# A linear-attention and token-selection kernel: q columns grouped by heads, and M in six passes

## The chip, the cores and the metric

The kernel runs on one core of one Trainium2 chip. The core has a matrix engine (TensorE, "PE" in the profile; its weight loads are listed as "PEld"), VectorE ("DVE"), ScalarE ("ACT"), GpSimd ("POOL"), and SyncE ("SP"), whose queue here issues most of the transfers (DMAs). Each engine works through its own instructions in the order in which they were written, and waits for others by semaphores. The metric is the device time of one execution in microseconds (us).

## The reference, cut to what matters

x holds 2048 tokens of 640 bfloat16 numbers. Three things are added: x, a linear attention A on the normalised x, and a block B that changes eight tokens only.

```python
xn = layernorm(x)
# A: 32 heads of 20 columns, wqkv is 640 x 1920, wo is 640 x 640
q, k, v = split_heads(xn @ wqkv)
phi = lambda t: where(t > 0, t + 1, exp(t)) + 1e-6
pq, pk = phi(q), phi(k)
kv  = einsum("bhsd,bhse->bhde", pk, v)      # 20 x 20 per head
z   = einsum("bhsd->bhd", pk)               # column sums
num = einsum("bhqd,bhde->bhqe", pq, kv)
den = einsum("bhqd,bhd->bhq", pq, z) + 1e-6
A = (num / den) @ wo
# B: the 8 tokens with the largest r = x @ w_r
y = (silu(x_sel @ w_gate) * (x_sel @ w_up)) @ w_down * sigmoid(r_sel)
B = x + scatter_add(y)
out = x + A + B
```

## The kernel before

The 2048 tokens are 16 tiles of 128. All of x stays on chip (x_sb), and so do the normalised tiles (xn), their transposes (xnT, features on the partitions), the feature maps pk (tokens on the partitions) and pqT (features on the partitions).

**The tile loop.** For each tile t TensorE computes k(t) (`k_mm`, L236, ten matmuls, with the router's column r appended to the weights), then a part of G = xn^T pk for the tile before (`ga_mm`, L259: three chunks of xn by 512 columns of pk), then q(t) (`q_mm`, L248). q comes out transposed: 25 matmuls of 128 columns have a slice of the weights as the stationary operand, `wq[:, kc, m::KC]`, every fifth column. So the 640 columns of q are dealt to five blocks m by their remainder modulo 5, and each block has four columns of each of the 32 heads. ScalarE takes exp and relu of the results (L213, L216), and VectorE combines them to phi (`phi_vec`, L225).

VectorE also takes the statistics of a later tile (`ln_stats`, L163 and L167), and normalises one (`ln_norm`, L191). From tile 4 on (LN_FAST), the small arithmetic between the two is GpSimd's: an add, two powers and a copy of one column (L171, L176, L178, L179). In iteration 5 (CATCH) statistics are taken for two tiles and two tiles are normalised, so that from there on a tile is normalised three iterations ahead of its use. From tile 3 on (PE_TR) a normalised tile is transposed by a DMA on SP's queue (L196). In VectorE's queue an iteration stands in the order: statistics, normalise, phi of q(t-1), phi of k(t).

GpSimd also makes small constants, spread over the iterations by `small_consts` (L306 to L321, and the masks of iteration 6 by `head_select`, L146 and L150). The loads of the later weights are spread over the iterations by `late_loads` (L343).

**Between the loop and the output.** Column sums z of pk (`z_mm`, L460) go through a small DMA onto the partitions; the rest of G follows (`gb1`, L489; `gb2`, L590). The top eight tokens are found by VectorE (candidates candm, pc on TensorE, then positions), gathered by GpSimd (xsT), and sent through B's matrices (gu, L606; py, L688). `pden` (L571) multiplies pqT by the masked z; its inverse rden goes to memory and comes back repeated on all partitions (rb), and `norm` multiplies pqT by it (L632). Then kv per block of 80 columns (`kv_mm`, `kv_evict`, L659 and L670) is written into kvT masked by heads, and M = kv wo is computed (L728): five blocks m, each with two halves of the output columns, two blocks of 80 accumulated one upon the other, and four head groups side by side in the array.

**Output.** For each tile ten matmuls of pqT by M (L743), then VectorE adds x_sb (L751), which has been written to memory (xcp), had y added there by an indirect DMA, and been read back. The result is stored by SP's or ScalarE's queue.

All orders are written out by hand; nothing is rescheduled.

Of the kernel before, what the change touches and what calls it, by code (L numbers as in the profile page):

```python
# [8 lines left out]
P = 128  # L9
# [16 lines left out]
PAD = 16  # L26
# [3 lines left out]
WARM = 10  # L30
LAST = (0, 320, 512, 640)
# [13 lines left out]
def kernel(  # L45
# [42 lines left out]
    wq = sb([P, KC, D], BF16, "wq")  # L88
    wv = sb([P, KC, D], BF16, "wv")
# [3 lines left out]
    kvT = sb([EB, PAD + NEB * KC * 2 * PAD], BF16, "kvT")  # L93
# [4 lines left out]
    rscr = dram.tile([NTB * P, TBLK], BF16, name="rscr")  # L98
# [55 lines left out]

    head_select(headg[:], [(0, NTB), (-4, H)], 1, 4)
# [87 lines left out]

    def q_mm(t, tag="B"):
        ps = pair(tag, f"q{t}")
        for m in range(KC):
            for kc in range(KC):
                nc.tensor.matmul(  # L248
                    ps[:, m * P : (m + 1) * P],
                    lhsT=wq[:, kc, m::KC],  # L250
                    rhs=xnT[:, kc, t * P : (t + 1) * P],
                    start=(kc == 0 and m in (0, 4)), stop=(kc == KC - 1),
                    skip_group_check=True,
                )
        return ps
# [47 lines left out]
    def small_consts(t):  # L303
        if t == 3:
            for j in range(4):
                nc.gpsimd.affine_select(  # L306
                    out=cmask[:], in_=cmask[:], compare_op=ALU.not_equal, fill=1.0,
                    base=-32 * j, pattern=[[-1, C]], channel_multiplier=1,
                )
        elif t == 4:  # L310
            nc.gpsimd.affine_select(
                out=selm[:], in_=selm[:], compare_op=ALU.not_equal, fill=1.0,
                base=0, pattern=[[-1, NTB]], channel_multiplier=1,
            )
# [26 lines left out]
    def late_loads(t):  # L341
        def part(dst, src, a, b):
            nc.sync.dma_start(dst[:, a:b, :], src[:, a:b, :])  # L343

        wv_v = wqkv_v[:, :, 2 * D : 3 * D]
        plan = {
            2: (x_sb, x_v, 8, 12), 5: (x_sb, x_v, 12, 16),
            6: (wg, kcF, 0, 2), 7: (wg, kcF, 2, 4), 8: (wg, kcF, 4, 5),
            9: (wu, kcU, 0, 2), 10: (wu, kcU, 2, 4), 11: (wu, kcU, 4, 5),
            12: (wv, wv_v, 0, 2), 13: (wv, wv_v, 2, KC), 14: (wo, wo_v, 0, 4), 15: (wo, wo_v, 4, 8),  # L350
            16: (wd, kcD, 0, 6), 17: (wd, kcD, 6, 12),
        }
        if t in plan:
            part(*plan[t])

# [12 lines left out]
    def q_phi(t, er):  # L368
        phi_vec(pqT[:, :, t * P : (t + 1) * P], er, True)
# [31 lines left out]
    for t in range(2, T):  # L401
# [18 lines left out]
        small_consts(t)  # L420
        late_loads(t)
# [20 lines left out]
    nc.vector.max(cand[:, 0, :], rT[:])  # L442
    nc.vector.max_index(idxu[:], cand[:, 0, :], rT[:])
# [28 lines left out]
    zpart = sb([P, D], F32, "zpart", tag="rb")  # L472
    nc.scalar.copy(zpart[:], zp[:, 0:D])
    zrel = sb([P, 4, KC], F32, "zrel")
    with nc.allow_non_contiguous_dma(reason="column sums from rows to partitions"):
        for i in range(4):
            (nc.sync if i < 3 else nc.scalar).dma_start(
                zrel[:, i, :], zpart[32 * i : 32 * i + 1, :].rearrange("o (p m) -> o p m", m=KC)
            )
    late_loads(T)  # L480
    late_loads(T + 1)
# [25 lines left out]
    for t in range(4, T):  # L507
        gb1(t)
# [22 lines left out]
    q_phi(T - 1, qer)  # L531
# [4 lines left out]
    for c in range(C):  # L536
# [7 lines left out]
        out=zm[:], in0=headg[:, 0, :].unsqueeze(1).to_broadcast([P, KC, H]),  # L544
# [19 lines left out]
    keep(T - 4, T)  # L564
    nc.scalar.copy(GT[:, 3:5, 0:TBLK], two(gbA[:]))
# [15 lines left out]
    nc.scalar.activation(rden[:], lden[:], AF.Exp, scale=-1.0)  # L581

# [20 lines left out]
    for a, w in enumerate((wg, wu)):  # L603
# [9 lines left out]
    sg = sb([P, FJ], F32, "sg")  # L613
# [5 lines left out]
    rb = sb([P, S], BF16, "rb")  # L619

    nc.sync.dma_start(
        rscr[:].rearrange("(p r) n -> p r n", r=4), rden[:].unsqueeze(1).to_broadcast([P, 4, TBLK])
    )
    for j in (0, 2):
        nc.sync.dma_start(
            rb[:, j * TBLK : (j + 2) * TBLK].rearrange("p (j n) -> p j n", j=2),
            rscr[j * P : (j + 2) * P, :].rearrange("(j p) n -> p j n", j=2),
        )

    def norm(j):  # L630
        sl = pqT[:, :, j * TBLK : (j + 1) * TBLK]
        nc.vector.tensor_tensor(  # L632
            out=sl, in0=sl,
            in1=rb[:, j * TBLK : (j + 1) * TBLK].unsqueeze(1).to_broadcast([P, KC, TBLK]),
            op=ALU.mult,
        )

    for t in range(2, 12):
        gb2(t)
# [8 lines left out]
    for t in range(12, T):  # L648
        gb2(t)
    nc.scalar.copy(GT[:, :, TBLK:D], gbC[:, 0:D].rearrange("p (c f) -> p c f", c=KC))  # L650


    pkv = (bank("D0", "pkv0"), bank("D1", "pkv1"), pair("B", "pkv2"))
    groups = ((0, 2, 4), (1, 3, 5), (6, 7))

    def kv_mm(i):
        for n, b in enumerate(groups[i]):
            for kc in range(KC):
# [8 lines left out]
    def kv_evict(i):  # L667
        n, w = len(groups[i]), KC * 2 * PAD
        lo, step = groups[i][0], groups[i][1] - groups[i][0]
        nc.vector.tensor_tensor(  # L670
            out=kvT[:, PAD : PAD + NEB * w].rearrange("e (b m c) -> e b m c", b=NEB, m=KC)[
                :, lo : groups[i][-1] + 1 : step, :, 0:PAD
            ],
            in0=pkv[i][0:EB, 0 : n * EB].rearrange("e (b c m) -> e b m c", b=n, m=KC),
            in1=mask80[:].rearrange("e m h j -> e m (h j)").unsqueeze(1).to_broadcast([EB, n, KC, PAD]),
            op=ALU.mult,
        )

    for i in range(3):
        kv_mm(i)  # L680
        kv_evict(i)
    norm(0)

# [19 lines left out]

    M = sb([P, KC, D], BF16, "M", tag="wq")
# [17 lines left out]
    for m in range(KC):  # L722
        pm = Acc("CBADC"[m], f"M{m}")
        for a, b in halves:
            for i in range(2):
                for g in range(4):
                    o = PAD + ((2 * g + i) * KC + m) * 2 * PAD - i * PAD
                    nc.tensor.matmul(  # L728
                        pm.at(a, b)[32 * g : 32 * g + 32, :],
                        lhsT=kvT[:, o : o + 2 * PAD],  # L730
                        rhs=wo[:, 2 * g + i, a:b],
                        start=(i == 0), stop=(i == 1),
                        tile_position=(0, 32 * g),
                    )
        copy = nc.vector.tensor_copy if m in (2, 4) else nc.scalar.copy
# [5 lines left out]

    def out_mm(t, ps, m, a, b):
# [4 lines left out]
            start=(m == 0), stop=(m == KC - 1),  # L747
# [5 lines left out]
    for t in range(T):  # L753
        o_t = work.tile([P, D], BF16, tag=("ek", "rk", "eq", "rq")[t % 4], name=f"o_t{t}")
        if t < T - 1:
            po = Acc("BADC"[t % 4], f"o{t}")
            for m in range(KC):
# [5 lines left out]
            if t == 4:  # L763
                norm(3)
        else:
            for i in range(3):
                a, b = LAST[i : i + 2]
                ps = pair("CBA"[i], f"o_last{i}")[:, 0 : b - a]
                for m in range(KC):
# [37 lines left out]
```

## Time and profile before

| | us |
|---|---|
| runs, median of 3 (lowest, highest) | 111.76 (111.65, 112.45) |
| the profiled execution's own time | 111.62 |
| its span in the profile | 109.9 |
| TensorE busy | 105.5 |
| VectorE busy | 86.1 |
| ScalarE busy | 55.1 |
| GpSimd busy | 37.9 |

How to read it: times in the trace count from the start of the span; the 1.7 us between span and time lie around it. Matmuls overlap in the engine's pipeline, so that the busy time of TensorE says only that something was in it, and the chain of work that ended last tells more: it is followed back from the last instruction, at each step to whatever released it, and shows on which engine each stretch of the time was spent. The granted TensorE clock is 1.00 in all stretches.

### The profile page before, as it was taken

How to read it: one execution, taken by the hardware profiler on the slowest of the kernel's cores; microseconds unless marked ns; L12 is line 12 of the kernel's file. 1: busy time of each engine (PE TensorE's matmuls, PEld its weight loads, DVE VectorE, ACT ScalarE, POOL GpSimd, SP SyncE). 2: the span in 40 equal slices, each digit the busy share in tenths (PEclk: the TensorE clock that was granted, in tenths of full speed). 3: DMA queues.
4: the chain of work that ended last, by engine and by line, in shares of the span. 5: the costliest groups of instructions: out<-in, count | busy, mean ns of one | idle time of the engine just before them, and what ended most of it. 6: DMA issues, size and time to landing. Idle time of an engine off the chain costs nothing.

```text
span 109.9 us, 2999 instructions
## 1 busy us (share of the span) xinstructions
PE 105.5 (96%) x1183; PEld 69.3 (63%) x1183; DVE 86.1 (78%) x205; ACT 55.1 (50%) x102; POOL 37.9 (34%) x83
## 2 busy tenths in 40 slices
PE   6998999999999999999999999999999999999990
PEld 2456866777577766777667744447995555555560
DVE  6889999887999889875999896951348967698680
ACT  4037987778867797777977745068028000000000
POOL 5414195989889955770000000240008100000000
DMA  2998164930569999998859970899541289997333
GB/s 72 335 375 292 33 36 75 283 66 3 118 177 321 220 267 280 316 305 224 290 187 285 292 257 5 232 378 372 175 145 51 15 228 323 340 387 277 128 119 119
DMA packets 25358, 23.09 MB, mean 210 GB/s; under 512 B 10624, under 2 KB 24064, under 8 KB 25344
## 3 DMA queue, kind: packets, MB, share of 16 engines
q1 hardware_dynamic: 22784, 20.43, 66.5%
q10 hardware_dynamic: 2384, 2.43, 6.4%
q8 instruction: 9, 0.15, 0.6%
q0 software_dynamic: 176, 0.04, 0.6%
q14 instruction: 5, 0.04, 0.1%
HBM read 14.94 MB, written 5.81 MB: 189 GB/s over the span
## 4 chain that ended last, share of the span: by engine, by line
PE 76%; DVE 10%; POOL 8%; issue 3%; DVEq 0%; POOLq 0%
PE o L743 14%; PE k L236 13%; PE q L248 13%; PE gbA L489 6%; PE gaC L259 5%; PE warm L271 4%; PE gbC L590 4%; POOL sq L176 3%; DVE st L163 2%; PE gaD L259 2%; DVE pk L225 2%; PE M L728 2%; POOL sc L178 2%; DVE xn L191 2%; PE gu L606 2%
## 5 line engine op out<-in xcount | busy, mean ns | idle before, releaser
L248 PEld LDWEIGHTS <-wq 128*128 128x128 bf16 x400 | 24.2, 117 | 3.4
L236 PE MATMUL k<-wk,xnT 128*128 128x512 bf16 (+1 forms) x160 | 24.8, 301 | 0.3 <-ACT xnT L206 0.3
L248 PE MATMUL q<-xnT,wq 128*128 128x128 bf16 x400 | 24.9, 220 | 0.0
L743 PEld LDWEIGHTS <-pqT 128*128 128x128 bf16 x165 | 12.8, 98 | 9.3
L236 PEld LDWEIGHTS <-xnT 128*128 128x128 bf16 x160 | 12.3, 98 | 8.5 <-ACT xnT L206 0.9
L213 ACT ACTIVATE eq<-q 128x640 bf16<-128x640 f32 x16 | 11.2, 703 | 10.5 <-PE q L248 10.5
L225 DVE SCALAR_TENSOR_TENSOR pk<-ek,rk 128x640 bf16<-128x640 bf16 x16 | 13.2, 824 | 3.6 <-ACT rk L216 3.4
L743 PE MATMUL o<-M,pqT 128*128 128x512 bf16 x110 | 15.8, 300 | 0.0
L176 POOL TENSOR_TENSOR sq<-sq,half 128x1 bf16<-128x1 bf16 x16 | 12.5, 778 | 6.2 <-DVE sc L175 4.0
L163 DVE BATCH_NORM_STATS2 st<-x_sb 128x6 f32<-128x320 bf16 x32 | 14.1, 480 | 0.4 <-DMA x_sb<-in_A_x_dram 0.4
L225 DVE SCALAR_TENSOR_TENSOR pqT<-eq,rq 128x640 bf16<-128x640 bf16 x16 | 13.2, 823 | 0.7 <-ACT rq L216 0.7
L213 ACT ACTIVATE ek<-k 128x640 bf16<-128x640 f32 x16 | 11.3, 705 | 1.6 <-PE k L236 0.4
L751 DVE TENSOR_TENSOR o_t<-o,x_sb 128x640 bf16<-128x640 f32 x11 | 8.8, 820 | 3.3 <-DMA x_sb<-xcp 1.7
L216 ACT ACTIVATE rq<-q 128x640 bf16<-128x640 f32 x16 | 11.2, 700 | 0.0
L216 ACT ACTIVATE rk<-k 128x640 bf16<-128x640 f32 x16 | 11.2, 699 | 0.0
L259 PE MATMUL gaC<-pk,xn 128*128 128x512 bf16 x32 | 9.5, 378 | 0.2 <-DVE pk L225 0.2
L537 POOL COPY xsT<-xnT 128x5 bf16 x8 | 1.9, 312 | 21.7 <-DVE icol L551 21.7
L178 POOL TENSOR_TENSOR sc<-sq,neg 128x1 f32<-128x1 bf16 x12 | 8.6, 716 | 0.9
L191 DVE TENSOR_SCALAR xn<-x_sb,sc 128x640 bf16<-128x640 bf16 (+2 forms) x17 | 6.9, 412 | 1.2 <-POOL sc L179 1.0
L489 PE MATMUL gbA<-pk,xn 128*128 128x512 bf16 x32 | 7.3, 380 | 0.0
L360 DVE TENSOR_TENSOR x_sb<-x_sb,xn 128x640 bf16<-128x640 bf16 x16 | 7.0, 482 | 0.0
L259 PEld LDWEIGHTS <-xn 128*128 128x128 bf16 x48 | 4.0, 97 | 4.1 <-issue 0.4
(152 smaller groups left out, 120.4 us busy)
## 6 DMA issues: line engine op xcount, KB each, us to landing
xcp<-x_sb SPq DMA_DIRECT2D x4, 640.0 KB, 5.2
x_sb<-in_A_x_dram SPq DMA_DIRECT2D x3, 640.0 KB, 4.7
wd<-in_B_w_down_dram SPq DMA_DIRECT2D x2, 960.0 KB, 6.6
x_sb<-xcp SPq DMA_DIRECT2D x3, 640.0 KB, 6.8
wg<-in_B_w_gate_dram SPq DMA_DIRECT2D x2, 768.0 KB, 6.6
wu<-in_B_w_up_dram SPq DMA_DIRECT2D x2, 768.0 KB, 5.3
out_dram<-o_t ACTq DMA_DIRECT2D x8, 160.0 KB, 2.7
out_dram<-o_t SPq DMA_DIRECT2D x7, 160.0 KB, 3.4
```

What stands on the lines that cost most here:

```text
L163: nc.vector.bn_stats(out=stat[t][:, h, :], in_=x_sb[:, t, h * HW : (h + 1) * HW])
L176: nc.gpsimd.tensor_tensor(out=sq[:, 1:2], in0=sq[:, 0:1], in1=half[:], op=ALU.pow)
L178: nc.gpsimd.tensor_tensor(out=sc[:, 1:2], in0=sq[:, 1:2], in1=neg1[:], op=ALU.pow)
L191: nc.vector.tensor_scalar(out=xn[:, t, a:b], in0=x_sb[:, t, a:b], scalar1=sc[:, 0:1], scalar2=sc[:, 1:2], op0=ALU.subtract, op1=ALU.mult,)
L213: nc.scalar.activation(e[:], ps[:, 0:D], AF.Exp)
L216: nc.scalar.activation(r[:], ps[:, 0:D], AF.Relu)
L225: nc.vector.scalar_tensor_tensor(out=dst, in0=ea, scalar=1.0, in1=ra, op0=ALU.min, op1=ALU.add)
L236: nc.tensor.matmul(ps[:, a:b], lhsT=xnT[:, kc, t * P : (t + 1) * P], rhs=wk[:, kc, a:b], start=(kc == 0), stop=(kc == KC - 1),)
L248: nc.tensor.matmul(ps[:, m * P : (m + 1) * P], lhsT=wq[:, kc, m::KC], rhs=xnT[:, kc, t * P : (t + 1) * P], start=(kc == 0 and m in (0, 4)) ...
L259: nc.tensor.matmul(gaC[:, c * TBLK : (c + 1) * TBLK] if c < 2 else gaD[:], lhsT=xn[:, t, c * P : (c + 1) * P], rhs=pk[:, t, 0:TBLK], start ...
L489: nc.tensor.matmul(gbA[:, (c - 3) * TBLK : (c - 2) * TBLK], lhsT=xn[:, t, c * P : (c + 1) * P], rhs=pk[:, t, 0:TBLK], start=(t == 0), stop ...
L743: nc.tensor.matmul(ps, lhsT=pqT[:, m, t * P : (t + 1) * P], rhs=M[:, m, a:b], start=(m == 0), stop=(m == KC - 1),)
```

## The change

The columns of q are dealt to the five blocks in another way. Of each head's 20 columns the first 8 go to main block c = 0, the next 8 to c = 1, each of 256 columns (32 heads), and the last 4 to a block of 128: 512 + 128 columns in a fixed order, which `regroup` describes as a view of 640 columns. Blocks 0 and 2 of pqT then belong to heads 0 to 15, blocks 1 and 3 to heads 16 to 31, and block 4 to all.

- q of tiles 0 to 6 (QTOK = 7) is computed with the tokens on the partitions, ten matmuls with the regrouped view of wq as moving operand. Its feature map pq is transposed by a DMA on SP's queue into pqT. Tiles 7 to 15 are computed transposed as before, from wqp, a regrouped copy of wq that GpSimd makes in iterations 2 to 6, two copies each.
- M in six passes: blocks 0 to 3 take one pass each, since each block has its heads in four blocks of 80 columns, and block 4 takes two. Before, each of five blocks took two.
- The head mask of z is now headm, made by selects in iterations 7 to 11; mask80 is smaller.
- The loads of the weights are in other iterations (wg from 3 on, wd in 10 and 11).
- The phi of the last q stands ahead of `max_index`. `pden` stands ahead of the last three tiles of gb1. gb2 is split: four chunks of nine tiles, then the first half of kv and py, then the other seven tiles and the fifth chunk.
- rden goes to memory once, and twelve loads repeat its rows (three for each quarter of the tokens); `norm` is two operations.
- The first four output tiles are copied out by ScalarE and then added to x_sb.

```diff
+    def regroup(ap):
+        v = ap.rearrange("p (h e) -> p h e", e=DH)
+        main = v[:, :, 0 : 2 * E8].rearrange("p h (c d) -> p c h d", c=2)
+        return (main, 0, TBLK), (v[:, :, 2 * E8 : DH], TBLK, D)
+
+    def wq_regroup(kc):
+        for src, a, b in regroup(wq[:, kc, :]):
...
+            nc.gpsimd.tensor_copy(wqp[:, kc, a:b].rearrange(pat, **kw), src)
...
     def q_mm(t, tag="B"):
         ps = pair(tag, f"q{t}")
-        for m in range(KC):
-            for kc in range(KC):
+        if t >= QTOK:
...
+                        lhsT=wqp[:, kc, m * P : (m + 1) * P],
+                        rhs=xnT[:, kc, t * P : (t + 1) * P],
...
+        for kc in range(KC):
+            for rhs, a, b in regroup(wq[:, kc, :]):
                 nc.tensor.matmul(
-                    ps[:, m * P : (m + 1) * P],
-                    lhsT=wq[:, kc, m::KC],
-                    rhs=xnT[:, kc, t * P : (t + 1) * P],
...
+                    ps[:, a:b],
+                    lhsT=xnT[:, kc, t * P : (t + 1) * P],
+                    rhs=rhs,
+                    start=(kc == 0), stop=(kc == KC - 1),
                 )
...
-            head_select(mask80[:], [(0, KC), (-DH, 4), (0, 4)], 1, DH)
+            head_select(mask80[:], [(-DH, 4), (0, E8)], 1, DH)
+        elif 7 <= t < 11:
+            m = t - 7
+            head_select(headm[:, m, m % 2, :], [(-E8, HV)], 1, E8)
+        elif t == 11:
+            head_select(headm[:, 4].rearrange("p i x -> p (i x)"), [(-E4, H)], 1, E4)
...
     def q_phi(t, er):
-        phi_vec(pqT[:, :, t * P : (t + 1) * P], er, True)
+        if t >= QTOK:
+            phi_vec(pqT[:, :, t * P : (t + 1) * P], er, True)
+            return
+        pq = work.tile([P, D], BF16, tag="pq", name=f"pq{t}", bufs=3)
+        phi_vec(pq[:], er, False)
+        nc.sync.dma_start_transpose(pqT[:, :, t * P : (t + 1) * P], pq[:])
...
         small_consts(t)
+        if 2 <= t < 2 + KC:
+            wq_regroup(t - 2)
         late_loads(t)
...
     nc.vector.max(cand[:, 0, :], rT[:])
+    q_phi(T - 1, qer)
...
-    for t in range(4, T):
+    for t in range(4, DEN_AT):
         gb1(t)
...
     nc.scalar.activation(rden[:], lden[:], AF.Exp, scale=-1.0)
+    for t in range(DEN_AT, T):
+        gb1(t)
+    nc.scalar.copy(GT[:, 3:5, 0:TBLK], two(gbA[:]))
...
-    for m in range(KC):
-        pm = Acc("CBADC"[m], f"M{m}")
-        for a, b in halves:
-            for i in range(2):
+    for m, tag, copy in (
+        (0, "C", nc.scalar.copy), (2, "A", nc.vector.tensor_copy), (1, "B", nc.scalar.copy),
+        (3, "D", nc.scalar.copy), (4, "C", nc.vector.tensor_copy),
+    ):
+        pm = Acc(tag, f"M{m}")
+        for x in (None,) if m < 4 else (0, 1):
+            for a, b in halves:
                 for g in range(4):
```

More of the change, by code (lines that the diff above doesn't have):

```diff
@@ L647, with kv_mm @@
     )
[L648 to L658, printed above, removed]
+    pkv = bank("D0", "pkv0"), bank("D1", "pkv1")
+    def kv_mm(i, ns, kcs=range(KC)):
+        for n in ns:
+            b = 4 * i + n
+            for kc in kcs:
                 nc.tensor.matmul(
@@ L667, in kv_evict @@
     def kv_evict(i):
[L668 to L682, printed above, removed]
+        src = pkv[i][0:EB, 0 : 4 * EB].rearrange("e (b h c) -> e b h c", b=4, h=4)
+        main = kvT[:, 256 * i : 256 * (i + 1)].rearrange("e (b c h d) -> e c b h d", b=4, c=2, h=4)
+        rest = kvT[:, 512 + 128 * i : 512 + 128 * (i + 1)].rearrange("e (b x) -> e b x", b=4)
+        for c in range(3):
+            w = E8 if c < 2 else E4
+            dst = main[:, c] if c < 2 else rest[:, :, 0:16].rearrange("e b (h d) -> e b h d", h=4)
+            nc.vector.tensor_tensor(
+                out=dst, in0=src[:, :, :, c * E8 : c * E8 + w],
+                in1=mask80[:, :, 0:w].unsqueeze(1).to_broadcast([EB, 4, 4, w]), op=ALU.mult,
+            )
+    kv_mm(0, range(4))
+    kv_evict(0)
     py = pair("A", "py")
@@ L702 @@
         nc.sync.dma_start(x_sb[:, a:b, :], xcp_v[:, a:b, :])
+    for t in range(GB_A, T):
+        gb2(t, gbC, range(4))
+    nc.scalar.copy(GT[:, 0:4, TBLK:D], gbC[:, 0:TBLK].rearrange("p (c f) -> p c f", c=4))
+    gbB = pair("B", "gbB")
+    for t in range(T):
+        gb2(t, gbB, (4,))
+    nc.scalar.copy(GT[:, 4, TBLK:D], gbB[:, 0:P])
+    norm(0)
+    kv_mm(1, (0, 1))
+    kv_mm(1, (2, 3), range(4))
+    kv_mm(1, (2, 3), (4,))
+    kv_evict(1)
     M = sb([P, KC, D], BF16, "M", tag="wq")
@@ L768 @@
                 ps = pair("CBA"[i], f"o_last{i}")[:, 0 : b - a]
-                for m in range(KC):
+                for m in M_ORDER:
                     out_mm(t, ps, m, a, b)
```

165 lines of the change are left out of this document (101 added, 64 removed).

## The prediction

> **What bounds the kernel now.** I read the page's shares first, then the chain that ended last in order of time, then the engine that the chain passes through before it turns to TensorE for good.
>
> ```profile
> PE 105.5 (96%) x1183; PEld 69.3 (63%) x1183; DVE 86.1 (78%) x205; ACT 55.1 (50%) x102; POOL 37.9 (34%) x83
> ...
> PE 76%; DVE 10%; POOL 8%; issue 3%; DVEq 0%; POOLq 0%
> ```
>
> TensorE sets the end, yet POOL, busy for a third of the span, holds 8% of the chain. The chain shows where:
>
> ```profile
> 27.29 0.15 POOL sc L179
> ...
> 27.47 0.45 DVE xn L191
> 27.92 0.73 DVE pqT L225
> 28.65 0.75 DVE pk L225
> ...
> 29.44 0.59 PE gaC L259 x2
> ...
> 33.67 1.40 PE q L248 x25
> 35.07 1.38 PE k L236 x10
> ```
>
> From 29.44 on TensorE works without a gap (the last two rows are q(7) and k(8); a tile is q 1.40, k 1.38, ga about 0.65: 3.43 us). Just before, it waited: POOL finishes the scale of tile 8 (sc), VectorE normalises tile 8, and only behind that, in VectorE's queue, come q's feature map and pk of tile 5, for which ga(5) waits. So in the first seven tiles POOL has no slack. Its own timeline (start, duration, operation, idle time before):
>
> ```profile
> 17.36 0.41 POOL L179 CAST sc<-mv 128x1 f32<-128x1 bf16 x1
> 18.86 0.30 POOL L171 TENSOR_SCALAR sq<-mv 128x1 bf16<-128x1 bf16 x1 [1.09 <-DVE mv L167]
> 19.24 1.00 POOL L176 TENSOR_TENSOR sq<-sq,half 128x1 bf16<-128x1 bf16 x1
> ...
> 25.98 0.57 POOL L176 TENSOR_TENSOR sq<-sq,half 128x1 bf16<-128x1 bf16 x1
> ...
> 27.26 0.18 POOL L179 CAST sc<-mv 128x1 f32<-128x1 bf16 x1
> ...
> 30.51 0.30 POOL L171 TENSOR_SCALAR sq<-mv 128x1 bf16<-128x1 bf16 x1 [0.43 <-DVE mv L167]
> ...
> 32.57 0.18 POOL L179 CAST sc<-mv 128x1 f32<-128x1 bf16 x1
> 32.71 0.43 POOL L146 TENSOR_SCALAR_AFFINE_SELECT mask<-mask 80x80 bf16<-80x80 bf16 x1
> 33.21 0.62 POOL L150 TENSOR_SCALAR_AFFINE_SELECT mask<-mask 80x80 bf16<-80x80 bf16 x1
> ```
>
> Between 18.86 and 33.83 POOL idles once, for 0.43 us.
>
> **The change, part by part.** *Regrouped weight copy.* Five pairs of POOL copies (128x512 and 128x128) stand behind the small constants of iterations 2 to 6. Pair 0 comes ahead of the scale of tile 6, pairs 1 and 2 ahead of tile 8's, pair 3 ahead of tile 10's, pair 4 behind the masks of iteration 6, and q(7) reads all five. The trace has no such copy; rows to bound it:
>
> ```profile
> 3.07 0.31 POOL L150 TENSOR_SCALAR_AFFINE_SELECT headg<-headg 128x128 bf16<-128x128 bf16 x1
> ...
> 21.62 1.63 POOL L306 TENSOR_SCALAR_AFFINE_SELECT cmask<-cmask 128x8 f32<-128x8 f32 x4
> ...
> 25.05 0.18 POOL L311 TENSOR_SCALAR_AFFINE_SELECT selm<-selm 4x4 f32<-4x4 f32 x1
> ```
>
> 128 elements cost 0.31 and 4 cost 0.18, about 1.05 ns an element: 0.18 + 512 x 1.05 = 0.71, and 0.31: 1.02 a pair with VectorE quiet. Beside VectorE, POOL is slower: the same power took 1.00 at 19.24 and 0.57 at 25.98, with these neighbours:
>
> ```profile
> 19.00 0.82 DVE L225 SCALAR_TENSOR_TENSOR pqT<-eq,rq 128x640 bf16<-128x640 bf16 x1
> ...
> 25.50 0.83 DVE L163 BATCH_NORM_STATS2 st<-x_sb 128x6 f32<-128x320 bf16 x2
> ...
> L176 POOL TENSOR_TENSOR sq<-sq,half 128x1 bf16<-128x1 bf16 x6 | 4.4, 735 | 0.5
> ```
>
> The last row is from the groups of 15.7 to 33.9 us: six powers, 735 ns on average. 735/570 is 1.3, so I take 1.3 a pair. Low bound: size free above 128 elements, 0.4 a pair. High bound: twice 1.02, as four selects of 8 elements took 1.63 (0.41 each, against 0.18 for selm): 2.0.
>
> [...]
>
> The sum: pair 0 overflows its gap (17.77 to 18.86) by 0.2; pairs 1 and 2 add 2.6; tile 8's scale is 2.8 late, hence norm(8), pk(5) and ga(5), which had no slack: ga(5) at 32.2. POOL ends the masks at 33.83 + 2.8 + 1.3 (pair 3) - 0.4 (idle filled) - 0.3 (mask 32 wide instead of 80) = 37.2, pair 4 at 38.5, q(7) some 0.15 later, against 33.67 in the chain: 5.0. VectorE stands still for 2.8 us of this, so POOL runs unhindered there; I take off 0.2: **+4.8 us**. The first wait lies inside the second. Afterwards POOL has, per tile, the four norm operations (2.2 for tile 10, 30.51 to 32.75) and two new selects, no dearer than the mask's 0.43 and 0.62: 3.3 of 3.43, so no further loss. Bounds by the same sum: +1.2 with 0.4 a pair, +8.6 with 2.0.
>
> *Token-major q, tiles 0 to 6.* Ten matmuls of 512 and 128 columns for 25 of 128: k's 1.38 for q's 1.40, -0.1 in all, before q(7)'s wait and so worth nothing. The moving operand is now read in runs of 8. No row shows that; the nearest is the strided weight load:
>
> ```profile
> L248 PEld LDWEIGHTS <-wq 128*128 128x128 bf16 x400 | 24.2, 117 | 3.4
> ...
> L236 PEld LDWEIGHTS <-xnT 128*128 128x128 bf16 x160 | 12.3, 98 | 8.5 <-ACT xnT L206 0.9
> ```
>
> 117/98 on seven tiles would be 7 x 1.38 x 0.19 = 1.8 us, also in front of the wait: hidden there, 1.8 if the wait is gone. The regrouped z sum reads so too: at most 0.2.
>
> *DMAs on SP.* Seven more transposes, and wg loads three tiles earlier:
>
> ```profile
> L196 SPq DMA_TRANSPOSE xnT<-xn x13: 1200/1207/2636, 12.1 to 49.5; - x13
> ...
> 22.07 0.39 DVE L191 TENSOR_SCALAR xn<-x_sb,sc 128x640 bf16<-128x640 bf16 x1
> ...
> 27.66 1.55 PE L236 MATMUL k<-wk,xnT 128*128 128x512 bf16 x10
> ```
>
> SP then issues two transposes and a load a tile, 1.2 + 1.2 + 0.6 = 3.0 of 3.43. The transpose of tile 6 (normalised at 22.46, wanted by k(6) at 27.66) may be late behind wg; up to 2.8 of that hides in ga(5)'s wait. Cost 0; about 1 without that cover.
>
> *M.* 80 matmuls become 48. The chain has both numbers:
>
> ```profile
> 66.60 0.13 PE pc L499
> ...
> 73.89 1.74 PE gu L606 x40
> ...
> 82.28 1.63 PE M L728 x48
> ...
> 85.00 2.82 PE o L743 x20
> ```
>
> 48 took 1.63, all 80 took 85.00 - 82.28 = 2.72: -1.1.
>
> *The stretch between.* The reordering takes covers away:
>
> ```profile
> 65.75 0.21 DVE L437 TENSOR_TENSOR candm<-split,selm 4x64 bf16<-4x64 bf16 x1
> ...
> 69.22 0.82 DVE L225 SCALAR_TENSOR_TENSOR pqT<-eq,rq 128x640 bf16<-128x640 bf16 x1
> ...
> 77.14 0.56 DVE L617 TENSOR_TENSOR hm<-gu,hm 128x384 bf16<-128x384 f32 x1
> ...
> 80.42 0.40 DVE L670 TENSOR_TENSOR kvT<-pkv,mask 80x240 bf16<-80x240 f32 x1 [1.48 <-PE pkv L659]
> ...
> 72.06 1.01 ACT L565 CAST GT<-gbA 128x1024 bf16<-128x1024 f32 x1 [4.32 <-PE gbA L489]
> ...
> 74.64 1.28 ACT L584 ACT_TABLE_LOAD   x1
> ```
>
> candm ended at 65.96, 0.64 before pc; q's last feature map (0.75 from start to the next start) now stands ahead of it: pc waits 0.1 to 0.2. pden comes 1.2 earlier, but the gbA eviction (1.01) and the table load (1.28) now lie behind the last gbA matmul, so hm is ready at about 77.5 and not 77.7, while its transpose is reached at 77.2 instead of 78.5: 0.3. The second kvT eviction (three operations, about 0.8 with the handover) is covered by only two M passes, 0.54: 0.3. Together +0.8, between 0 and 2 (M copies and loads of rb late). Evicting the first four output tiles by ScalarE and an earlier reload of x_sb relieve VectorE, which is not on the chain there: 0.
>
> Sum against this execution's 111.62 us (span 109.9 and 1.7 around it): 111.6 + 4.8 - 1.1 + 0.8 = **116.1**. The runs' median, 111.76, is 0.1 above it, so 116.2 on their scale.
>
> **Rivals.** *Not slower: POOL makes room.* Copies at 0.7 a pair (size half as dear), and the norm operations, moved to where VectorE is quiet, at 0.57 for 0.73: two powers in six tiles give 12 x 0.16 = 1.9 back. Then q(7) comes at 38.65 - 3.0 - 1.9, about 33.7, no later than before, and M's 1.1 less 0.8 remains: 111.3; 110.5 if the covers hold too. It decides where five pairs cost less than about 3.5 us. Against it: no idle time on POOL, and powers of 1.00 beside the feature maps, which still run twice a tile.
>
> *Copies blocked:* 2.0 a pair gives 119.9. For it: 0.41 a select.
>
> *TensorE slows down after its wait.* Its first matmuls were slow:
>
> ```profile
> L271 PE MATMUL warm<-zero 128*128 128x512 bf16 x10 | 4.4, 632 | 1.0 <-DVE zero L117 1.0
> ```
>
> Ten of 512 columns took 4.4 us, 0.44 each; later k's ten, five of 512 and five of 129, take 1.38, which is 0.22 for 512. The wait before ga(5) is 3.2 us: 0.4 from k(6)'s end (27.66 + 1.38) to 29.44, and 2.8. If it brought that pace back for a tile, 3.4 us of work would take 6.8; 2.4 are hidden before q(7), 1.0 is not, and a second such wait adds up to 1.7: 117 to 119. [...]
>
> *The change doesn't do what it says:* six passes wait for kvT and copies and take the old 2.7: 117.2.
>
> **How the numbers follow.** The forecast, a pair between 0.8 and 1.7 us: 113.6 to 118.3, chance 0.60. POOL makes room 0.16; copies blocked 0.12; slow TensorE 0.07; M gains nothing 0.05. About 1% is what a measurement of this kernel can tell from no change. Faster by over 1% wants free copies and held covers: 0.07; within 1%, the rest of the first rival: 0.10; slower 0.83. The range leaves out one in ten on each side: 112.3 (the low bound of a pair with the stretch's 0.8) to 119.5.
>
> **What would show it.** Right: ga(5) starting near 32 behind sc and xn, q(7) waiting for the POOL copy, pairs of 1.0 to 1.6 us, 3.43 a tile afterwards, M in 1.6 us plus a wait. Wrong: no gap on TensorE before tile 8, or copies under 0.5 us.

## The result, and the profile after

| | before | after |
|---|---|---|
| median of the runs, us (lowest, highest) | 111.79 (111.65, 112.45), 4 runs | 115.42 (115.29, 115.70), 4 runs |
| ratio, 95% interval | | 1.032 (1.028 to 1.036) |
| the profiled execution's own time, and its span | 111.62, 109.9 | 115.7, 114.0 |

The kernel is 3.2% slower; 116.1 was forecast. The total was right, but not its terms, as this section and the runs show. (The ratios leave out executions more than 1.5% above the fastest of their kernel, two of e9_pq_later's six and two of e11_combined's thirteen; the profiled one of e11_combined is such a one, so its rows are not read.)

First the page of after: the shares of the engines, and the chain that ended last.

```profile
PE 104.9 (92%) x1034; PEld 63.7 (56%) x1046; DVE 86.7 (76%) x215; ACT 58.5 (51%) x108; POOL 43.0 (38%) x101
...
PE 54%; POOL 16%; DVE 14%; DMA 5%; issue 4%; ACT 3%; SPq 1%; POOLq 0%; DVEq 0%; ACTq 0%
```

TensorE does 0.6 us less than before, and its share of the chain falls from 76% to 54%; POOL's doubles from 8% to 16%. So the loss is waiting. What TensorE waited for, in before (engine, line, who released it; us in total, times, longest):

```profile
PE warm L271 <- DVE zero L117: 1.0, 1, 1.0
PE k L236 <- ACT xnT L206: 0.3, 1, 0.3
PE gaC L259 <- DVE pk L225: 0.2, 1, 0.2
```

The same view of after:

```profile
PE warm L301 <- DVE zero L125: 1.0, 1, 1.0
PE o_last L807 <- DVE o_t L815: 0.9, 1, 0.9
PE q L269 <- POOL wqp L262: 0.8, 1, 0.8
PE k L245 <- ACT eq L222: 0.8, 1, 0.8
PE pden L613 <- DVE zm L587: 0.6, 1, 0.6
PE gaC L289 <- DVE pk L234: 0.4, 1, 0.4
PE ph L689 <- DVE hm L659: 0.3, 1, 0.3
PE k L245 <- ACT xnT L215: 0.3, 1, 0.3
```

Five waits are new and one, gaC's, is longer. Those of q, ph and gaC stood in the prediction, k's only as a possibility, and those of pden and o_last not at all. Where they lie in time, from the chain of after:

```profile
28.60 0.14 POOL sc L188
...
35.45 0.57 POOL wqp L262
36.06 1.34 PE q L269 x21
...
64.82 0.32 PE pr L472 x4
...
68.56 0.61 SPq L524
69.22 3.68 DMA zrel<-zpart
...
73.77 1.26 PE pden L613 x20
...
86.00 0.93 PE M L791 x24
...
87.96 0.38 PE o L807 x2
```

Against the chain of before (pr at 62.48, M at 82.28, the output at 85.00, the end at 109.9) the 4.1 us of span fall into four parts:

| stretch | before | after | difference | forecast |
|---|---|---|---|---|
| start to pr (the tile loop) | 62.48 | 64.82 | +2.3 | +4.8 |
| pr to M | 19.80 | 21.18 | +1.4 | +0.8 (with 0.3 inside M) |
| M to the output | 2.72 | 1.96 | -0.8 | -1.1 |
| output to the end | 24.9 | 26.0 | +1.1 | 0 |

GpSimd's copies are these, in its timeline of after (pairs, x2: start, duration; then the four selects of cmask, which took 1.63 in before):

```profile
17.63 0.84 POOL L262 COPY wqp<-wq 128x512 bf16<-128x512 bf16 x2
...
22.01 0.94 POOL L262 COPY wqp<-wq 128x512 bf16<-128x512 bf16 x2
...
26.18 0.94 POOL L262 COPY wqp<-wq 128x512 bf16<-128x512 bf16 x2
...
31.33 0.94 POOL L262 COPY wqp<-wq 128x512 bf16<-128x512 bf16 x2
...
35.40 1.49 POOL L262 COPY wqp<-wq 128x512 bf16<-128x512 bf16 x2
```

```profile
21.11 0.97 POOL L336 TENSOR_SCALAR_AFFINE_SELECT cmask<-cmask 128x8 f32<-128x8 f32 x4
```

A pair took 0.84 to 0.94, not 1.3, and the selects of cmask 0.97 instead of 1.63. So tile 8's scale ended at 28.74 in the chain, 1.3 later than in before and not 2.8. Taken singly, the copy of 128x512 took 0.60 or 0.61 in all five pairs, that of 128x128 0.29 to 0.39 in four and 0.94 in the fifth, beside VectorE's feature map, which itself took 1.46 instead of 0.82 there. The matmuls of q(7) that had waited went on at 36.06, right behind the first copy of the fifth pair, which ended at 36.01; the slow second one, which they need only at their end, cost nothing:

```profile
35.28 1.46 DVE L234 SCALAR_TENSOR_TENSOR pq<-eq,rq 128x640 bf16<-128x640 bf16 x1
```

### The profile page after: what moved, and what is told of

Read it like the earlier page. It is cut to its first block, busy times and chain, and to the rows that moved or that the text cites. A ratio compares the mean times of both kernels' runs of the same rounds, so it can differ in the third digit from the quotient of the medians.

```text
span 114.0 us, 2786 instructions
## 1 busy us (share of the span) xinstructions
PE 104.9 (92%) x1034; PEld 63.7 (56%) x1046; DVE 86.7 (76%) x215; ACT 58.5 (51%) x108; POOL 43.0 (38%) x101
## 4 chain that ended last, share of the span: by engine, by line
PE 54%; POOL 16%; DVE 14%; DMA 5%; issue 4%; ACT 3%; SPq 1%; POOLq 0%; DVEq 0%; ACTq 0%
PE o L807 14%; PE q L269 11%; PE k L245 10%; POOL sq L185 5%; DVE st L172 4%; PE gaC L289 3%; DMA zrel<-zpart 3%; POOL wqp L262 3%; POOL sc L187 3%; POOL sq L180 3%; DVE xn L200 2%; DMA x_sb<-in_A_x_dram 2%; PE gaD L289 2%; DVE o_t L815 2%; PE gbC L635 1%
## 5 line engine op out<-in xcount | busy, mean ns | idle before, releaser
L245 PEld LDWEIGHTS <-xnT 128*128 128x128 bf16 x160 | 12.3, 98 | 10.5 <-DMA xnT<-xn 1.5
L807 PE MATMUL o<-M,pqT 128*128 128x128 bf16 (+1 forms) x117 | 16.8, 297 | 0.2
L269 PEld LDWEIGHTS <-wqp 128*128 128x128 bf16 x225 | 13.3, 98 | 3.1 <-POOL wqp L262 1.0
L269 PE MATMUL q<-xnT,wqp 128*128 128x128 bf16 x225 | 14.2, 219 | 0.8 <-POOL wqp L262 0.8
L279 PE MATMUL q<-wq,xnT 128*128 128x512 bf16 x70 | 11.0, 303 | 0.0
L815 DVE TENSOR_TENSOR o_t<-o,x_sb 128x640 bf16<-128x640 f32 x9 | 7.2, 823 | 3.2 <-PE o L807 3.2
L581 POOL COPY xsT<-xnT 128x5 bf16 x8 | 1.2, 217 | 20.7 <-DMA zrel<-zpart 20.7
L279 PEld LDWEIGHTS <-xnT 128*128 128x128 bf16 x70 | 5.6, 96 | 5.2
L187 POOL TENSOR_TENSOR sc<-sq,neg 128x1 f32<-128x1 bf16 x12 | 7.5, 627 | 0.9
L180 POOL TENSOR_SCALAR sq<-mv 128x1 bf16<-128x1 bf16 x12 | 6.6, 548 | 2.9 <-DVE mv L176 2.9
L234 DVE SCALAR_TENSOR_TENSOR pqT<-eq,rq 128x640 bf16<-128x640 bf16 x9 | 7.3, 817 | 0.2 <-ACT rq L225 0.2
```

The lines of the kernel that those rows point to most:

```text
L180: (nc.vector if t < LN_FAST else nc.gpsimd).tensor_scalar(out=sq[:, 0:1], in0=mv[:, 1:2], scalar1=EPS_BF16, scalar2=None, op0=ALU.add)
L187: nc.gpsimd.tensor_tensor(out=sc[:, 1:2], in0=sq[:, 1:2], in1=neg1[:], op=ALU.pow)
L234: nc.vector.scalar_tensor_tensor(out=dst, in0=ea, scalar=1.0, in1=ra, op0=ALU.min, op1=ALU.add)
L245: nc.tensor.matmul(ps[:, a:b], lhsT=xnT[:, kc, t * P : (t + 1) * P], rhs=wk[:, kc, a:b], start=(kc == 0), stop=(kc == KC - 1),)
L269: nc.tensor.matmul(ps[:, m * P : (m + 1) * P], lhsT=wqp[:, kc, m * P : (m + 1) * P], rhs=xnT[:, kc, t * P : (t + 1) * P], start=(kc == 0 a ...
L279: nc.tensor.matmul(ps[:, a:b], lhsT=xnT[:, kc, t * P : (t + 1) * P], rhs=rhs, start=(kc == 0), stop=(kc == KC - 1),)
```

## The experiments

Starts in this table are those of TensorE's own timeline (up to 0.17 ahead of the chain's), the waits in brackets those ahead of the instruction, all in us. Every ratio is to runs of the kernel before on the same chip.

| kernel | pr | pden | ph | M | output | end | ratio (95%) |
|---|---|---|---|---|---|---|---|
| before | 62.41 | 71.96 | 78.36 | 82.11 | 84.93 | 109.9 | 1 |
| after | 64.75 | 73.77 (0.60) | 80.62 (0.32) | 85.93 | 87.89 | 114.0 | 1.032 (1.028 to 1.036) |
| e1_tags | 64.85 | 74.11 (0.84) | 80.96 (0.33) | 86.27 | 88.23 | 113.4 | 1.029 (1.026 to 1.031) |
| e2_no_copies | 63.55 | 72.45 (0.48) | 79.30 (0.33) | 84.61 | 86.52 | 112.6 | 1.026 (1.021 to 1.032) |
| e4_loads_back | 64.98 | 73.61 (0.20) | 80.45 (0.32) | 85.75 | 87.72 | 113.8 | 1.035 (1.032 to 1.038) |
| e5_copies_alone | 64.52 | 74.07 | 80.47 | 84.22 | 87.04 | 113.2 | 1.027 (1.021 to 1.033) |
| e9_pq_later | 64.62 | 74.97 (1.92) | 81.91 (0.33) | 87.22 | 89.18 | 115.3 | 1.046 (1.040 to 1.053) |
| e6_qtok9 | 65.86 | 74.22 | 81.07 (0.33) | 86.37 | 88.33 | 114.5 | 1.036 (1.029 to 1.042) |
| e7_zflat | 65.49 | 73.94 | 80.79 (0.33) | 86.09 | 88.06 | 114.1 | 1.031 (1.027 to 1.035) |
| e10_stretch | 64.98 | 74.20 | 80.91 (1.05) | 86.21 | 88.17 | 114.3 | 1.037 (1.033 to 1.041) |
| e12_combined_now | 63.74 | 72.96 | 78.76 | 84.06 | 86.02 | 111.2 | 1.015 (1.011 to 1.018) |
| e13_later11 | 62.85 | 72.06 | 77.86 | 83.17 | 85.12 | 110.1 | 1.000 (0.999 to 1.002) |
| e14_den13 | 62.74 | 71.09 | 77.44 | 82.85 | 84.80 | 109.7 | 0.997 (0.995 to 0.999) |

**The loop: copies or transposes?** *The copies taken out.*

```diff
-        if 2 <= t < 2 + KC:
-            wq_regroup(t - 2)
...
-                        lhsT=wqp[:, kc, m * P : (m + 1) * P],
+                        lhsT=wq[:, kc, m * P : (m + 1) * P],
```

> The changed kernel without GpSimd's ten regrouping copies; tiles 7 to 15 read contiguous blocks of wq, so that the columns of q are in another order there and the output is not the reference's. All else stays, the seven transposes of pq and the earlier loads too. Theory (copies delay GpSimd's chain, and transposes on SP delay xnT under that cover): q(7)'s wait and GpSimd's share of ga(5)'s wait go, the late transposes of tiles 5 and 6 remain; the four transposes pr begin at 63.3 to 63.8 us in the span and not at 64.82, the time falls by 1.0 to 1.5 us. Rival A (the copies alone, as predicted): pr begins at 62.5, the time falls by 2.3. Rival B (transposes and loads alone): pr stays at 64.5 or later, the time stays within 0.3.

pr comes at 63.55, in the forecast stretch, 1.2 earlier than in after, and the median time is 1.1 less, though the intervals of the two ratios overlap. 1.14 us over before remain, and TensorE's timeline shows them:

```profile
24.70 1.56 PE L245 MATMUL k<-wk,xnT 128*128 128x512 bf16 x10 [0.31 <-DMA xnT<-xn]
29.07 1.56 PE L245 MATMUL k<-wk,xnT 128*128 128x512 bf16 x9 [0.74 <-ACT eq L222]
```

These are k(5) and k(6). Where the matmul's row names ScalarE, the weight load in front of it (the row of its group below, same kernel) waited for the transposed tile:

```profile
L245 PEld LDWEIGHTS <-xnT 128*128 128x128 bf16 x160 | 12.2, 98 | 10.9 <-DMA xnT<-xn 2.0 <-ACT xnT L215 0.8
```

*The copies put into the kernel before.* The same ten, but written to wd[:, kc, :], which is loaded later there:

```diff
+        if 2 <= t < 2 + KC:
+            wq_regroup(t - 2)
         late_loads(t)
```

> The kernel before with the ten copies added at the places of the changed kernel, written into the still unused tile wd, and read by nobody. Theory: with pairs of 0.94 us the scale of tile 8 is 1.3 us late and ga(5) with it; later scales have three iterations of lead and q(7) waits for nothing: pr begins at 63.8 (+1.3), the time is 112.9 to 113.4 against 111.8. Rival (the copies cost only through q(7)'s wait): pr at 62.5 to 62.8, no change within 0.3 us. [...]

pr comes 2.1 later than in before, more than forecast, and TensorE waited once:

```profile
31.24 0.59 PE L270 MATMUL gaC<-pk,xn 128*128 128x512 bf16 x2 [2.16 <-DVE pk L225]
```

That is ga(5) behind sc and xn of tile 8, the first of the two waits of the prediction. It is longer than forecast because GpSimd was slower here than in after: the second pair took 1.50 (its copy of 128x128 0.95, beginning 0.03 behind a feature map), and the selects of cmask 1.63. So copies alone cost 2.1, transposes alone 1.1, both together 2.3: they lie over one another. The other 1.2 us of this run's time came in the output stage, where VectorE's additions waited longer than in before for x_sb read back (0.93, 1.53 and 1.23 against 0.86, 0.77 and 0.86); why it landed late there was not tried.

*The loads of the weights back in before's iterations.*

```diff
-            2: (x_sb, x_v, 8, 12), 3: (wg, kcF, 0, 2), 4: (x_sb, x_v, 12, 16), 5: (wg, kcF, 2, 4),
+            2: (x_sb, x_v, 8, 12), 5: (x_sb, x_v, 12, 16),
+            6: (wg, kcF, 0, 2), 7: (wg, kcF, 2, 4), 8: (wg, kcF, 4, 5),
...
```

> The changed kernel with the loads of the weights in the iterations of the kernel before. Theory (the copies set q(7), the late transposes lie under them): the waits for xnT before k(5) and k(6) shrink from 1.5 us in all to under 0.5, yet q(7) still begins its main part near 36.0 and pr near 64.8: the time stays within 0.4 us of 115.4. Rival (loads and transposes set the first wait and all that follows): pr at 63.8 or earlier, the time falls by 1 us.

The time is that of after, as expected, but k(5) still waits, 0.81 us where under 0.5 was expected, and pr is at 64.98: the earlier wg loads are not what makes xnT late. That leaves the added transposes, which the next run moves.

*The transposes of pq seven iterations later.*

```diff
-        pq = work.tile([P, D], BF16, tag="pq", name=f"pq{t}", bufs=3)
-        phi_vec(pq[:], er, False)
-        nc.sync.dma_start_transpose(pqT[:, :, t * P : (t + 1) * P], pq[:])
+        phi_vec(wd[:, t, :], er, False)
...
-            10: (wd, kcD, 0, 6), 11: (wd, kcD, 6, 12), 12: (wo, wo_v, 0, 4), 13: (wo, wo_v, 4, 8),
+            10: (wo, wo_v, 0, 4), 11: (wo, wo_v, 4, 8), 14: (wd, kcD, 0, 6), 15: (wd, kcD, 6, 12),
```

> The changed kernel, but the seven transposes of pq are issued in iterations 7 to 13 instead of 0 to 6 (pq is kept in the space of wd meanwhile; wd is loaded in iterations 14 and 15, wo in 10 and 11). Theory 'the copies and the transposes each set a wait, and the two lie partly over one another': k(5) and k(6) no longer wait for xnT (0.76 and 0.7 us in the changed kernel), but q(7) still waits for GpSimd's last copy, at about 36, so that the first matmul of pr comes at 64.0 to 64.8 (64.8 in the changed kernel, 62.5 in the kernel before) and the time falls by at most 0.8 us, to 114.7 or more. Rival 'the two add up': leaving out the copies gave 1.3 us of the 2.3, so taking the transposes out of the way gives the other 1.1: pr at 63.7, time 114.3 or less.

In TensorE's timeline no k waits for xnT any more, and pr is at 64.62, only 0.13 earlier:

```profile
30.61 0.59 PE L290 MATMUL gaC<-pk,xn 128*128 128x512 bf16 x2 [1.53 <-DVE pk L235]
35.93 1.35 PE L270 MATMUL q<-xnT,wqp 128*128 128x128 bf16 x21 [0.84 <-POOL wqp L263]
74.97 1.36 PE L617 MATMUL pden<-pqT,zm 128*32 128x512 bf16 x20 [1.92 <-DVE zm L591]
```

The first theory holds for the loop: GpSimd's waits take the place of the others, and the copies cost 2.2 with the transposes out of the way. For the time it said at most 0.8 less, and by the ratios it became about 1.6 more: the loads of wd were still under way when the small transfers of z were issued, which landed after 5.3 us instead of 3.0 (median of those on SP, from issue), and pden waited 1.92. That loss belongs to the experiment's own edit, not to the change.

*q token-major up to tile 8.*

```diff
-QTOK = 7
+QTOK = 9
```

> The changed kernel with tiles 0 to 8 token-major (QTOK = 9), so that the first reader of the copies is q(9), some 6.9 us later than q(7). Theory 'the last copy is late for q(7), and not for q(9)': the wait of 0.84 us before q(7) is gone and nothing waits at q(9); pr at 63.9 to 64.2, time 0.6 to 0.9 us less than the changed kernel's. Rival 'the added transposes are the limit': two more of them on SP's queue make k(7) or k(8) wait for xnT, pr at 64.6 to 65.3 and no gain.

The wait for the copies is gone, as the theory had it, but the rival decides: three k wait for xnT instead, and pr is 1.1 later. TensorE's timeline:

```profile
24.75 1.56 PE L245 MATMUL k<-wk,xnT 128*128 128x512 bf16 x10 [0.22 <-DMA xnT<-xn]
29.77 1.56 PE L245 MATMUL k<-wk,xnT 128*128 128x512 bf16 x10 [1.39 <-DMA xnT<-xn]
55.48 1.56 PE L245 MATMUL k<-wk,xnT 128*128 128x512 bf16 x10 [1.31 <-DMA xnT<-xn]
```

**The tail: where the last tile is accumulated.** In after the last tile's first part takes bank pair C, which tile 14 holds too ("ABCD"[14 % 4] is C; before, "BADC" put it in D), so it waits until VectorE has added tile 14.

```diff
-                ps = pair("CBA"[i], f"o_last{i}")[:, 0 : b - a]
+                ps = (bank("D0", "o_last0"), bank("D1", "o_last1"), pair("A", "o_last2"))[i][:, 0 : b - a]
```

> The changed kernel, with the last tile's three parts in banks that were freed several tiles earlier (D0, D1 and A in place of C, B, A). Theory (a PSUM reuse at the end): the 0.92 us in which the last tile's first matmul waits for VectorE's addition of tile 14 goes, and the time falls by 0.8 to 1.0 us, 115.4 to about 114.5. Rival (the output stage is longer because it starts badly, behind M's copies): the wait moves to VectorE's additions at the end and the time stays within 0.3 us of 115.4.

The row in TensorE's timeline of after, and the one that answers to it in this run:

```profile
109.36 1.53 PE L807 MATMUL o_last<-M,pqT 128*128 128x320 bf16 x15 [0.92 <-DVE o_t L815]
```

```profile
108.62 1.53 PE L807 MATMUL o_last<-M,pqT 128*128 128x320 bf16 x15
```

Output to end is 25.2 us instead of 26.1, against 25.0 in before. The table bears it out: every kernel with the old banks has 26.0 to 26.2 there (e5, built on before, aside), every one with the new banks 24.9 to 25.2. The time fell by only 0.5; in the profiled execution pden waited 0.84 instead of 0.60 and pr came 0.1 later.

**The stretch.** *Column sums copied without the permutation.*

```diff
-        zpart[:].rearrange("a (p m) -> a m p", m=KC), zp[:, 0:D].rearrange("a (m p) -> a m p", m=KC)
+        zpart[:], zp[:, 0:D]
```

> The changed kernel with the column sums copied out without the permutation (one contiguous copy, as in the kernel before). The sums then reach other partitions than they belong to, so the output isn't the reference's; amount of work and transfers are the same. Theory 'the permuted copy makes pden late': the copy takes 0.69 instead of 1.32 us, the sums land 0.6 earlier, pden's wait of 0.60 for zm is gone, and the time falls by 0.4 to 0.6 us. Rival 'the landing of the sums is slow in itself (3.7 instead of 2.2 us, whatever the copy)': pden still waits 0.3 or more and the time falls by less than 0.3.

The copy in ScalarE's timeline, after and then this run:

```profile
67.21 1.32 ACT L518 COPY zpart<-zp 128x640 f32<-128x640 f32 x1 [1.06 <-PE zp L505]
```

```profile
67.95 0.69 ACT L518 COPY zpart<-zp 128x640 f32<-128x640 f32 x1 [1.06 <-PE zp L505]
```

0.63 less, pden no longer waits, and pr to pden falls from 9.02 to 8.45. But k(6) waited longer in this execution (pr at 65.49), and the time, with 1.031 against 1.032, doesn't resolve the gain: shown in the stage, not in the time.

*pden behind two more tiles of gb1, the sigmoid's table ahead of the eviction of gbA.*

```diff
-DEN_AT = 13
+DEN_AT = 15
...
-    nc.scalar.copy(GT[:, 3:5, 0:TBLK], two(gbA[:]))
-
     warm_s = sb([P, 1], F32, "warm_s")
     nc.scalar.activation(warm_s[:], eps6[:], AF.Sigmoid)
+    nc.scalar.copy(GT[:, 3:5, 0:TBLK], two(gbA[:]))
```

> The changed kernel with two orders in the stretch between loop and output altered: pden stands ahead of the last tile of gb1 instead of the last three (DEN_AT 15), and the load of the sigmoid's table stands ahead of the eviction of gbA instead of behind it. Theory 'the stretch lost 0.6 before pden and 0.3 before ph because the reorder took their cover away': pden waits 0.2 or less, ph does not wait for hm, M starts 0.6 to 0.9 us earlier after pr, and the time falls by 0.5 to 0.9 us. Rival 'the waits move on' (rden later by 0.4 us, so rb and with it the products of M and the output, or the table load behind rden holds up the eviction): the time falls by less than 0.3 us.

The rival is right. pden has no wait, but ph waits 1.05 instead of 0.32. ScalarE's timeline of this run shows what sets ph:

```profile
75.51 0.69 ACT L622 ACTIVATE lden<-pden,eps 128x512 f32<-128x512 f32 x1 [3.87 <-PE pden L613]
76.23 0.63 ACT L623 ACTIVATE rden<-lden 128x512 bf16<-128x512 f32 x1
76.88 1.28 ACT L627 ACT_TABLE_LOAD   x1
...
78.28 0.99 ACT L628 CAST GT<-gbA 128x1024 bf16<-128x1024 f32 x1
79.17 0.49 ACT L656 ACTIVATE sg<-gu 128x384 f32<-128x384 f32 x1
```

From pden's end to the sigmoid's ScalarE has 4.2 us of work in a row, in whatever order; pden later means ph later. To shorten it the eviction has to leave ScalarE, which the next kernel tries.

**All mended.** The losses named so far, each with its remedy, in one kernel: QTOK 5; two pairs of copies in GpSimd's idle time ahead of tile 4's statistics, the other three in iterations 2 and 3, cmask's selects in iteration 11; the transposes of pq six iterations later; wd loaded behind the column sums; pden ahead of the last tile of gb1, gbA evicted by VectorE; the new banks of the last tile.

```diff
-QTOK = 7
+QTOK = 5
+LATER = 6
...
     ln_norm(3)
+    wq_regroup(2)
+    wq_regroup(3)
     ln_stats(4)
...
-    nc.scalar.copy(GT[:, 3:5, 0:TBLK], two(gbA[:]))
+    nc.vector.tensor_copy(GT[:, 3:5, 0:TBLK], two(gbA[:]))
```

> The changed kernel with every loss that the runs so far showed mended at once: tiles 0 to 4 token-major instead of 0 to 6; GpSimd's copies for blocks 2 and 3 of the rows moved ahead of the statistics of tile 4, where GpSimd was idle from 10.7 to 13.2, the other three in iterations 2 and 3, and the selects of cmask moved from iteration 3 to 11; the transposes of pq issued six iterations later (from the space of wd); wd loaded behind the column sums, as in the kernel before; pden ahead of the last tile of gb1, and the eviction of gbA on VectorE, so that the sigmoid's table and hm come earlier; the last tile's parts in banks that no addition still holds. Theory 'these are the losses': no wait before k, ga or q later than the start-up, pr at 62.0 to 62.8 (62.4 in the kernel before, 64.8 in the changed one), pden and ph wait 0.2 or less, M in 2.0, no 0.9 before the last tile; time within 1% of the kernel before (111.0 to 112.4 if that is at 111.7). Rival 'the five transposes alone are enough to make k late': pr at 63.2 or more, and over 1% slower than before.

Ratio 1.0025 (1.0006 to 1.0045), median 112.0 against 111.6: within 1% of before, as the theory said of the time; what it said of the single waits is not read here. The same with each transpose of pq issued at once:

> As the one with everything mended, but each transpose of pq is issued as soon as pq is there, as in the changed kernel (tiles 0 to 4 only). Theory 'a transpose of pq ahead of a transpose of xn on SP's queue makes k(5) and k(6) late': k(5) or k(6) waits for xnT, pr at 62.8 to 63.6, 0.5 to 1.0 us more than with the transposes moved. Rival 'with GpSimd relieved, xn comes earlier and hides the transposes': no wait, the same pr as with the transposes moved.

It takes 1.2% more. TensorE's timeline has three waits for the late tiles:

```profile
25.01 1.56 PE L245 MATMUL k<-wk,xnT 128*128 128x512 bf16 x10 [0.74 <-ACT eq L222]
28.80 1.56 PE L245 MATMUL k<-wk,xnT 128*128 128x512 bf16 x10 [0.19 <-DMA xnT<-xn]
32.80 1.56 PE L245 MATMUL k<-wk,xnT 128*128 128x512 bf16 x10 [0.40 <-DMA xnT<-xn]
```

The two kernels differ only in when pq's transposes are issued (and in where pq is kept until then), so their place in SP's queue is worth that 1.2%. Put behind nearly all of xn's:

```diff
-LATER = 6
+LATER = 11
```

> The version with every known loss mended, but the five transposes of pq are issued in iterations 11 to 15 (behind nearly all of xn's) instead of 6 to 10. Theory 'every transpose of pq that stands ahead of one of xn on SP's queue can make a k late': k(11) to k(13) no longer wait for xnT (1.0 and 0.2 us in the profiled execution with 6 to 10), pr at 62.2 to 62.8, time 0.3 to 0.8 us less than with 6 to 10, that is 111.1 to 111.6 where the kernel before takes 111.6. Rival 'the transposes of xn are slow by themselves behind the loads of the weights': k still waits, no gain.

No k waits for a transposed tile any more, and in the view of transfers the transposes of xn land after 3.2 us (median, from issue), where it was 3.9 in before, 5.7 in after and 5.1 in e12; here the row of e13, then that of after:

```profile
xnT<-xn SPq DMA_TRANSPOSE x13, 3.2
```

```profile
xnT<-xn SPq DMA_TRANSPOSE x13, 5.7
```

pr is at 62.85, 0.05 past the forecast stretch, and the time equals that of before; ga waits 0.6 in all, against 0.2 in before. The gain over e11 is 0.2%, less than forecast, and the two intervals overlap. Last, pden ahead of three tiles again:

```diff
-DEN_AT = 15
+DEN_AT = 13
```

> As the one with pq's transposes in iterations 11 to 15, and pden ahead of the last three tiles of gb1 again (as in the changed kernel) instead of the last one. Theory 'ScalarE's chain from pden to the sigmoid sets ph, and with the sums landing early pden need not wait': pden 0.9 us earlier without a wait, ph without the 0.3 us that it waited for hm; 0.2 to 0.4 us less than with pden ahead of the last tile. Rival 'the sums land too late for it': pden waits 0.3 or more, and the time is the same or more.

pden starts 1.0 earlier without a wait, ph does not wait, and the kernel takes 111.46 against 111.69: 0.3% less than before, the only kernel here whose interval lies below 1. M's saving is kept (1.95 from M to the output, against 2.82 in before), while the loop is still 0.3 longer and the stretch from pr to M 0.4.

## Why the prediction was right in its total and wrong in its terms

- **POOL copies, +4.8: the mechanism right, the size wrong.** The chain is as told: ga(5) behind sc and xn of tile 8, then q(7) behind the last copy, and 3.43 a tile afterwards (k(8) to k(9), 37.24 to 40.67). The failing step is "I take 1.3 a pair": 0.84 to 0.94 was measured for four and 1.49 for the fifth. The factor of 1.3 for VectorE's company was not needed, since all four pairs ran beside VectorE's work; the slope "1.05 ns an element" came from a select, and 0.61 and 0.29 for copies of 512 and 128 give 0.83; and the selects of cmask came out 0.66 us cheaper. Redone with these, the scale is 1.2 late and not 2.8, and the masks end at 35.3 and not 37.2 (measured 1.3 and 35.45). That q(7) must wait for the whole of the last pair was wrong too: one copy of 0.61 was enough, so that its main part came at 36.06 and not 38.65, 2.4 behind the 33.67 of before. The copies alone cost 2.1 (e5) or 2.2 (e9). The low bound, "0.4 a pair", did not follow from its rows: two copies at the 0.31 of 128 elements are 0.6, which gives +2.1 by the same sum and not +1.2.
- **Copies blocked: fell.** The rival had 2.0 for every pair; four of after's took 0.84 to 0.94, the fifth 1.49, and in e5 two of the five were long (1.50 and 1.44). Single operations did run long beside VectorE's. At 35.28 two were long at once: the feature map, 1.46 for 0.82, and the copy of 128x128, 0.94 where the four others took 0.29 to 0.39. The operation of L178 (L187 of after) that runs shortly before the selects took 1.20 in before, where it began 0.03 behind a feature map, and 0.55 in after, where it began 0.01 ahead of one. What made them long was not shown.
- **DMAs on SP, 0, about 1 without cover: right.** Without the copies the transposes cost 1.14 (e2), with them 0.13 (e9). The cover was in the end the wait of q(7), as ga(5) itself waited only 0.38. That wg's loads would be what makes the tile late was wrong (e4): the transposes of pq are.
- **Token-major q, nothing: right.** The moving operand in runs of 8 cost nothing: its 512-column matmuls took 387 ns on average against 381 for k's in before (group below, of after). The bound of 1.8 us from the strided weight load was far too wide.

```profile
L279 PE MATMUL q<-wq,xnT 128*128 128x512 bf16 x35 | 10.6, 387 | 0.0
```

- **M, -1.1: right in the work, short by a wait.** 1.96 instead of 2.72. The wait for the second kvT eviction, 0.3 in the stretch's sum, did not come: each block needs only its own of the three operations, and blocks 0, 2, 1 and 3 begin 0.27 to 0.28 apart (block 3 is M3a). Block 4 begins 0.48 behind block 3, and so 0.2 late. It takes bank pair C again, which ScalarE empties of block 0 (first of two copies below, ended at 87.18, 0.05 ahead of block 4). In before block 4 took block 0's bank too, but each block lasted twice as long (0.54 against 0.27) and covered the copy. The rows of after, from the timelines of TensorE (two), ScalarE and VectorE:

```profile
86.75 0.39 PE L791 MATMUL M3a<-wo,kvT 80*32 80x512 bf16 x4
...
87.23 0.73 PE L791 MATMUL M<-wo,kvT 80*32 80x512 bf16 x16
...
86.49 1.29 ACT L799 CAST M<-M 128x640 bf16<-128x640 f32 x2 [0.95 <-PE M L791]
...
86.03 0.62 DVE L718 TENSOR_TENSOR kvT<-pkv,mask 80x128 bf16<-80x128 f32 x3 [2.19 <-PE pkv L703]
```

- **The stretch, +0.8: undersized.** Without the 0.3 for kvT, which stood inside M, 0.5 was forecast and 1.4 came, within the bounds of 0 to 2. pc waited for nothing and ph for 0.32, as forecast. Left out was pden: its cover of three tiles of gb1 was given away while the permuted copy (0.63 more) and slower landing sums came ahead of it. Either remedy removes the wait: the plain copy (e7), or sums that are there earlier, with the permuted copy and pden in the same place (e14: issued at 66.55, and VectorE adds them up at 69.75 without a wait, where in after it was 68.56 and, behind a wait of 1.3, 73.1; in e6 pden doesn't wait either). The two waits make 0.9 of the 1.4; without either, e14 still takes 0.4 more than before from pr to M, and why stays open.
- **Output, 0: wrong.** 1.1 us. I read the change of who evicts the first four tiles, and not the new letters of the bank rotation, which put tile 14 and the last tile into one pair.
- **TensorE slower after its wait: not seen.** After 36.06, behind a wait of 0.84, a tile takes 3.43 us at once, though no wait here was as long as the rival's 3.2: the longest in these runs' rows is 2.16 (e5).

The errors were -2.5 in the loop, +0.9 in the stretch and +1.1 in the output; M with the 0.3 for kvT came out at the -0.8 that the two gave together, by another wait. The total was met by luck: the errors cancel.

## What to carry to other kernels

Two causes that made the same engine late did not add: the smaller lay almost wholly under the larger (1.1 and 2.1 alone, 2.3 together), so a run that removes one shows only what it sticks out by. The transposes of pq cost their place in the queue: issued at once (e12), they let xn's land after 5.1 us, and three k waited (0.74, 0.19 and 0.40); behind nearly all the transfers that matmuls wait for (e13), they let xn's land after 3.2, and no k waited for one. When a rotation of accumulators is relabelled, follow every letter to the end of the kernel: the last tile had no cover for a shared pair (0.92), and halving M's passes uncovered the copy out of another (0.2).

## What was not expected of the hardware

- For four times the elements a GpSimd copy took 1.6 to 2.1 times as long in after: 0.60 or 0.61 us for 128x512 against 0.29 to 0.39 for 128x128, but for the 0.94 of the one beside the long feature map. The averages differ from run to run, as a long one may be among either size: 608 and 478 ns in after, 848 and 344 in e12.
- ScalarE's copy of 128x640 f32 took 1.32 us with the output written at a stride of five elements (after), and 0.69 in a row (e7).
- The 2.5 KB transfers of z landed after 2.2 us (before), 3.0 (after) or 5.3 (e9; medians of those on SP). In the view of windows (the last two columns are the mean busy share of the DMA queues and GB/s) the stretch from 68 to 70 us, in which they were issued in after (68.56) and e9 (68.43), stands at 0.05 and 1.06. So in e9 bulk was still under way beside them; in after it was not, and why one of the four took 3.7 there stays open.

```profile
68.00:70.00 2.00, 2.00 (x12) 0.78 (x11) 1.52 (x9) 0.73 (x2) 0.00 (x0) 1.00 0.05 12
```

```profile
68.00:70.00 2.00, 2.00 (x11) 0.81 (x10) 1.52 (x10) 0.73 (x2) 0.00 (x0) 1.00 1.06 393
```
